# Two tokens per partition for q and k, another order of the loads, and more token halves in tile 1

## The chip, the cores and the metric

The kernel runs on one core of one Trainium2 chip. The metric is the device time of one execution in microseconds (us); before the change the median of five runs is 304.95 us (304.39 to 306.18). The engines are TensorE (PE, matrix multiplies), VectorE (DVE), ScalarE (ACT), GpSimd (POOL, which here issues the loads) and SyncE (SP, which issues the stores).

## The reference

What is computed is attention with a sliding window of 64 tokens, and then two layers with a SiLU between them on its result. There are 8 batches of 576 tokens (4608 in all), 8 heads of 64, d_model 512 and d_ff 2048. The inputs and the output are float32.

```python
rel = pos[:, None] - pos[None, :]
scores = np.where((rel >= 0) & (rel < 64), q @ k.T / sqrt(64), -1e9)
attn = softmax(scores) @ v                       # per batch and head
x = attn.transpose(0, 2, 1, 3).reshape(4608, 512)
h = x @ w_in
out = (h / (1 + exp(-h))) @ w_out
```

## The kernel before

Everything is one program whose order is made by a small planner in the kernel itself (the class `Plan`, lines 15 to 119). The functions `add_...` hand it operations with a class, an assumed duration for each engine that may run them, what they depend on, and, for work that writes PSUM, a pool of banks. `Plan.run` goes through an assumed time line: whenever an engine is free it takes, by rank, an operation whose dependencies have been seen. Then the operations are emitted in that order. The assumed durations are therefore costs in a plan; on the chip each engine runs its own list in order, and waits on semaphores where something is late. For a load that GpSimd issues, the plan adds to the transfer a time until it is seen: 1.2 us in the first 40 us of the plan, and 3.2 us after (line 102). No more than eight such loads are under way at once.

**Loads.** q, k, v, w_in and w_out are loaded by GpSimd's queue, which casts float32 to bfloat16 on the way; stores of the output go over SyncE. Batch 0's q and k come in large pieces and are turned by PE. For batches 1 to 7, `load_rows` (line 239) brings one head of q or k into 32 partitions of a `nat` tile: 18 tokens per partition, with partition p holding tokens p, 32 + p, 64 + p and so on. So the piece that lies together in DRAM is one token of one head, 64 elements. Four such loads fill one tile with four heads. `turn_blocks` (line 244) then has VectorE transpose it in blocks of 32 by 32 into `qt` or `kt`, in two instructions per tile: each takes half of the 18 token groups, and both halves of a head's 64 elements. A batch has four such tiles: q and k of heads 0 to 3 (group 0), q and k of heads 4 to 7 (group 1).

**Order of the loads.** After batch 0's inputs come the ten pieces of w_in. Then `SECOND_LOADS` (line 139) gives the order for batch 1, one letter at a time: `a` is q and then k of group 0 (eight loads), `b` those of group 1, `w` the next of the eight pieces of w_out (two d_ff blocks of 128 each), and `v` one of the four pieces of v. The pieces of w_out that are left follow. Later batches load `a`, `b` and then v. In this text w0 to w7 are the pieces of w_out and v0 to v3 those of batch 1's v.

**Attention.** A batch has three groups of 192 tokens. For each, PE makes the scores in four banks (48 small matmuls, line 333), ACT takes the exponent (line 339), VectorE applies the mask (line 342), and PE multiplies with v (48 small matmuls, line 351; called pv below). VectorE then takes a reciprocal (358), normalises (361) and transposes the result into `bridge` (365). The halves of v are first copied to a second place by VectorE (lines 299 and 301). PSUM has eight banks: `at` is banks 0 to 3, `mp` banks 4 to 7, and `pv` banks 4 and 5. In batch 1 pv takes its two banks from `at`, from batch 2 on from `pv` (line 508).

**The two layers.** Nine tiles of 512 tokens. In tile j, the first layer (line 371) makes 16 d_ff blocks, four matmuls of 512 tokens each, and ACT applies SiLU (line 377) from PSUM into a `g` tile. The second layer (line 380) has 64 matmuls: 16 d_ff blocks times four groups of 128 tokens. In tile 0 the d_ff blocks are the outer loop, so that w_out is used piece by piece, eight matmuls for each; all four `mp` banks are then held until the end. In tiles 0 and 1 the first `FIRST` = 6 d_ff blocks are made in two parts of the tokens, all first parts before all second parts, since the tokens of the second part come later out of attention: in tile 1 tokens 0 to 255 need the first group of batch 1, and tokens 256 to 511 all three. `add_tile` (line 530) writes this down in `work`.

PE's list in this part reads, in order: first layer of tile 0; second layer of tile 0, with the three score groups and the three pv of batch 1 in between; first layer of tile 1; then scores of batch 2 within the second layer of tile 1, and so on, tile by tile.

Of the kernel before, what the change touches and what calls it, by code (L numbers as in the profile page):

```python
# [14 lines left out]
class Plan:  # L15
# [31 lines left out]
    def run(self):  # L47
        head = {c: 0 for c in self.queues}
        engines = sorted({e for q in self.queues.values() for op in q for e in op["us"]})
        free = {e: 0.0 for e in engines}  # L50
        can = {e: [c for c, q in self.queues.items() if any(e in op["us"] for op in q)] for e in engines}
        table, left = "exp", self.count
        pipe, sent = {True: 1.8, False: 0.0}, []
        events, order = [0.0], []
        while left:
            if not events:
                raise RuntimeError([(c, head[c], q[head[c]]["n"]) for c, q in self.queues.items() if head[c] < len(q)])
            now = self.now = heapq.heappop(events)
            while events and events[0] == now:
                heapq.heappop(events)  # L60
            moved = True
            while moved:
                moved = False
                for e in engines:
                    if free[e] > now:
                        continue
                    best, kept = None, set()
                    heads = [(self.queues[c][head[c]], c) for c in can[e] if head[c] < len(self.queues[c])]
                    for op, c in sorted(heads, key=lambda x: x[0]["first"]):
                        if e == "POOL" and op["dma"] and len(sent) >= 8 and sent[-8] > now:  # L70
                            continue
                        if e not in op["us"] or not self.done(op["deps"]) or (op["gate"] and not op["gate"]()):
                            continue
                        if op["pool"]:
                            idle = [i for i in self.pools[op["pool"]] if i not in kept and self.done(self.banks[i])]
                            if len(idle) < len(op["untils"]):
                                if op["pool"] != "mp":
                                    kept.update(self.pools[op["pool"]])
                                continue
                            idle.sort(key=lambda i: (op["pool"] == "mp" and i in self.pools["pv"],  # L80
                                                     max([u["seen"] for u in self.banks[i]], default=0.0)))
                            op["bank"] = idle[:len(op["untils"])]
                            for i, until in zip(op["bank"], op["untils"]):
                                self.banks[i] = until
                        best = (op, c)
                        break
                    if best is None:
                        continue
                    op, c = best
                    head[c] += 1  # L90
                    us = op["us"][e]
                    if op["table"] and op["table"] != table:
                        table, us = op["table"], us + 1.28
                    end = free[e] = now + us
                    soft = e == "POOL"
                    if op["dma"] is None:
                        op["seen"] = end + op["lat"]
                    elif soft:

                        begin = max(pipe[True], end + 1.4)  # L100
                        pipe[True] = begin + op["dma"] * (1.5 if pipe[False] > begin else 1.0)
                        op["seen"] = pipe[True] + op["lat"] + (1.2 if now < 40 else 3.2)
                        sent.append(op["seen"])
                        heapq.heappush(events, op["seen"])
                    else:
                        begin = max(pipe[False], end + 1.0)
                        busy = pipe[True] > begin
                        pipe[False] = begin + op["dma"] * (1.6 if busy else 1.0)
                        if busy:
                            pipe[True] += 0.6 * op["dma"]  # L110
                        op["seen"] = pipe[False] + {"ld0": 1.2, "st": 1.2}.get(c, 3.0)
                    op["at"], op["cls"], op["by"] = now, c, e
                    order.append((op, e))
                    left -= c != "warm"
                    moved = True
                    heapq.heappush(events, end)
                    heapq.heappush(events, op["seen"])
        for op, e in order:
            op["fn"](e)
# [3 lines left out]
def kernel(ctx, tc, q, k, v, w_in, w_out, out):  # L123
    nc = tc.nc
    B, H, S, D = q.shape
# [1 line left out]
    assert (B, H, S, D) == (8, 8, 576, 64) and (d_model, d_ff) == (512, 2048)  # L127
    NP = H // 2
    NB = S // 64
    NR = S // 32  # L130
    NG = 3
    NDC = d_model // 128
    NFT = d_ff // 128
    TT = 512
# [1 line left out]
    TB = TT // 64  # L136
    NK = 2
    NN, NNB, NE, NOT, NGT = 8, 8, 12, 4, NFT + 3
    FIRST, SECOND_LOADS = 6, "awbwvwvvwv"
    FIRST_LOADS = [(x[0], int(x[1])) for x in "q0 k0 q1 k1 q2 q3 k2 k3 v0 v1 v2 v3".split()]  # L140
    NOX, NRC, NV = 6, 6, 3
    NIV = 2
    NM0, MARGIN = 9, 1.3
# [16 lines left out]
    nats = [keep.tile([128, 2 * S], BF16, name=f"nat{i}") for i in range(NN)]  # L160
# [15 lines left out]
    p = Plan(  # L176
        {"at": range(4), "pv": range(4, 6), "mp": range(4, 8), "all": range(8)},
        rank=dict(prime=-8, early=-10, one=-9, first=-9, dma=-1, ld0=-1, st=-2, silu=-3, out=-2, pv=0, s=1, moe=99, warm=200, turn=2,
                  norm=0, inverse=0, bridge=0, exp=1, mask=1, lift=2, block=2, shift=2, cast=4, late=5, clear=9),
        rank0=dict(turn=-6, cast=-6, lift=-5, shift=-4.5, exp=-4, mask=-4, inverse=-3.5, norm=-3, bridge=-3.2),  # L180
        ahead=dict(s=-5.5, exp=-4.6, pv=-5.5, inverse=-4.3, norm=-4.2, bridge=-4.25),
    )
# [55 lines left out]

    def load_rows(i, b, a, kk, h):
        nc.gpsimd.dma_start(  # L240
            out=nats[i][32 * h:32 * h + 32].rearrange("p (r d) -> p r d", r=NR),
            in_=(q, k)[kk][b, 4 * a + h].rearrange("(r p) d -> p r d", p=32))

    def turn_blocks(i, b, a, kk, part):

        n = NR // 2
        to = kt[b % NK][:, 64:] if kk else qt[b % NK]
        nc.vector.transpose(  # L248
            out=to[:, 2 * a * S:2 * a * S + 2 * S].rearrange("x (s r t) -> x s r t", s=2, r=NR)[:, :, n * part:n * part + n],
            in_=nats[i].rearrange("p (r s d) -> p s r d", r=NR, s=2)[:, :, n * part:n * part + n],  # L250
        )

    def load_v(e, b, part):
# [141 lines left out]
    kq_done, v_done, s_last, pv_last = {}, {}, {}, {}  # L395
    nat_free = {}
# [15 lines left out]
    n_nat = [0, 0]  # L412
# [31 lines left out]

    def add_batch_qk(b):
        busy = s_last.get(b - NK, []) + ([c_k[b % NK]] if b < NK else [])
        for what in SECOND_LOADS if b < NIV else "ab":
            if what == "w":
                add_w_out([len(wout)])
            elif what == "v":  # L450
                add_v_loads(b, [len(v_landed.get(b, []))], [c_vv[b]])
            else:
                add_four(b, "ab".index(what), busy)

    def add_four(b, a, busy):
        kq_done[(b, a)] = []
        for kk in range(2):
            i = n_nat[0] % NN
            n_nat[0] += 1
            ld = [p.add("dma", {"POOL": 0.72}, lambda _, i=i, kk=kk, h=h: load_rows(i, b, a, kk, h), nat_free.get(i, []),  # L460
                        dma=0.52, lat=MARGIN) for h in range(4)]
            nat_free[i] = [p.add("block", {"DVE": 0.75}, lambda _, i=i, kk=kk, part=part: turn_blocks(i, b, a, kk, part),
                                 ld + busy, b=b) for part in range(2)]
            kq_done[(b, a)] += nat_free[i]

    def add_v_loads(b, parts, busy):
        v_landed.setdefault(b, []).extend(
# [19 lines left out]
    def add_unit(b, g, which, n0):  # L487
        whole = b > 0
        first = "0" if b == 0 and g == 0 else ""
        na = len(which)  # L490
# [8 lines left out]
        for i in range(2 * na):  # L499
# [3 lines left out]
            if b:  # L503
# [1 line left out]
            ready.append(ex)  # L505
        g_mask.append(ready)
        pv = p.add("pv" + first, {"PE": 0.1 + 0.22 * na}, None, ready + [d for a in which for d in v_done[(b, a)]], lat=0.1,
                   pool="pv" if b > 1 else "at" if b else "all", b=b, nb=na)

        def run_values(_):  # L510
            for i, a in enumerate(which):
# [18 lines left out]
    def add_tile(j):  # L530
# [5 lines left out]
        if j == 0:  # L536
            work = [(ft, lo, hi) for lo, hi in ((0, 192), (192, TT)) for ft in range(FIRST)] + work[FIRST:]
        elif j == 1:
            work = [(ft, lo, hi) for lo, hi in ((0, 256), (256, TT)) for ft in range(FIRST)] + work[FIRST:]
        for i, (ft, lo, hi) in enumerate(work):  # L540
            have = [op for n in range((j * TT + hi + 191) // 192) for op in o_done[n]]
            g, si = gt[ft]
# [98 lines left out]
```

## Time and profile before

One execution was profiled. It took 304.39 us, the fastest of the five; its span, from the first instruction to the last, is 302.6 us. PE's granted clock is 1.00 in it throughout.

| What (profiled execution) | us |
|---|---|
| time of the execution | 304.39 |
| span | 302.6 |
| PE busy | 290.6 |
| DVE busy / ACT busy / POOL busy | 138.5 / 171.7 / 125.1 |
| second layer's matmuls (L380), 608 shown | 130.7 busy, 368 ns mean |
| first layer's matmuls (L371), 624 shown | 128.3 busy, 362 ns mean |
| SiLU (L377), 156 | 86.2 busy, 564 ns mean |
| q and k loads (L240), 112 issues, 72 KB each | 75.2 on POOL, 0.68 mean |
| v loads (L255), 32 issues, 144 KB each | 33.2 on POOL, 1.05 mean |
| transposes of q and k (L248), 56 | 39.6 on DVE, 0.75 mean |

How to read it: a matmul's duration runs from its start to its modelled end, while the next one starts before that; the second layer's follow each other at 0.2186 us (64 in 13.99 us). Sizes of loads are those of the bfloat16 that lands; twice as many bytes are read. Lines of a timeline give start, length, engine, line and operation, the tiles written and read, and how many instructions were merged; in brackets stands the idle time of the engine before them and what ended it. "DMA to landing" is counted from the start of the issuing instruction to the last of the transfer's completions.

### The profile page before, as it was taken

The numbers are of one execution on the slowest core, as the hardware profiler recorded it, in microseconds if no ns is written. First come the engines' busy times: TensorE is split into PE (matmuls) and PEld (weight loads), VectorE is DVE, ScalarE is ACT, GpSimd is POOL, SyncE is SP. The second block draws the span as 40 slices with busy tenths as digits, with TensorE's granted clock in tenths as the row PEclk, the third lists the DMA queues.
The fourth block names the chain that finished last, engine by engine and source line by source line (L and its number), as shares of the span: only waits on it lengthen the run. The fifth ranks groups of instructions, "written<-read, shape, count | busy, mean of one in ns | idle before, by whom it ended". The sixth has DMA issues, their size and how long they took to land.

```text
span 302.6 us, 8339 instructions
## 1 busy us (share of the span) xinstructions
PE 290.6 (96%) x3564; PEld 142.9 (47%) x3564; DVE 138.5 (46%) x330; ACT 171.7 (57%) x313; POOL 125.1 (41%) x177
## 2 busy tenths in 40 slices
PE   4999879999999999999999999999999999999996
PEld 2555334654544454445444454445444544444444
DVE  2592568843998198606960885066105520000000
ACT  4686462667357735774487538763767366226611
POOL 8966985989999979990320000000000000000000
PEclk9999999999999999999999999999999999999999
DMA  8999999999999999994490110001000110010012
GB/s 172 161 168 160 138 164 176 186 171 112 178 182 141 113 171 148 163 116 80 65 95 2 38 71 35 3 37 71 35 2 37 71 37 0 35 69 37 1 69 73
DMA packets 115238, 28.64 MB, mean 95 GB/s; under 512 B 104704, under 2 KB 110464, under 8 KB 115200
## 3 DMA queue, kind: packets, MB, share of 16 engines
q0 software_dynamic: 109440, 18.07, 79.5%
q1 hardware_dynamic: 5760, 10.03, 9.1%
q8 instruction: 28, 0.46, 0.6%
q14 instruction: 10, 0.08, 0.1%
HBM read 36.70 MB, written 9.44 MB: 152 GB/s over the span
## 4 chain that ended last, share of the span: by engine, by line
PE 83%; POOL 9%; DMA 6%; issue 1%; ACT 0%; POOLq 0%; ACTq 0%
PE mp L380 40%; PE mp L371 37%; DMA w_in_sb<-in_moe_w_in_dram 3%; PE at L333 3%; PE mp L351 3%; POOL vv L255 3%; DMA w_out_sb<-in_moe_w_out_dram 3%; POOL w_in_sb L261 2%; POOL nat L240 2%; POOL natb L230 1%; POOL w_out_sb L267 1%; PE at L351 0%; ACT g L377 0%; POOL ident L189 0%; ACT ot L386 0%
## 5 line engine op out<-in xcount | busy, mean ns | idle before, releaser
L380 PE MATMUL mp<-w_out_sb,g 128*128 128x512 bf16 (+2 forms) x608 | 130.7, 368 | 3.3 <-DMA w_out_sb<-in_moe_w_out_dram 3.3
L371 PE MATMUL mp<-bridge,w_in_sb 128*128 128x512 bf16 (+3 forms) x624 | 128.3, 362 | 1.4 <-DVE bridge L365 0.7
L377 ACT ACTIVATE g<-mp 128x512 bf16<-128x512 f32 (+3 forms) x156 | 86.2, 564 | 33.6 <-PE mp L371 32.5
L371 PEld LDWEIGHTS <-w_in_sb 128*128 128x128 bf16 x624 | 60.2, 97 | 67.9 <-issue 8.0
L380 PEld LDWEIGHTS <-g 128*128 128x128 bf16 x608 | 55.8, 98 | 63.1 <-issue 2.9
L386 ACT COPY ot<-mp 128x512 f32<-128x512 f32 (+2 forms) x36 | 20.1, 563 | 64.2 <-PE mp L380 51.0
L342 DVE TENSOR_TENSOR e<-e,mask 128x384 bf16<-128x384 bf16 x84 | 25.9, 349 | 61.5 <-ACT e L339 60.9
L339 ACT ACTIVATE e<-at 128x384 bf16<-128x384 f32 x90 | 37.2, 495 | 20.1 <-PE at L333 19.8
L240 POOL DMA_DIRECT2D nat<-in_k_dram x56 | 37.5, 678 | 10.8 <-DMA vv<-in_v_dram 3.1
L240 POOL DMA_DIRECT2D nat<-in_q_dram x56 | 37.7, 683 | 3.1 <-DMA w_in_sb<-in_moe_w_in_dram 2.1
L255 POOL DMA_DIRECT2D vv<-in_v_dram x32 | 33.2, 1050 | 12.6 <-PE mp L351 12.6
L365 DVE STREAM_TRANSPOSE bridge<-ox 128x384 bf16<-128x384 bf16 x48 | 24.7, 552 | 0.0
L248 DVE STREAM_TRANSPOSE qt<-nat 128x576 bf16<-128x576 bf16 x28 | 19.8, 747 | 7.8 <-DMA nat<-in_q_dram 7.8
L248 DVE STREAM_TRANSPOSE kt<-nat 128x576 bf16<-128x576 bf16 x28 | 19.8, 745 | 2.0 <-DMA nat<-in_k_dram 1.8
L361 DVE TENSOR_TENSOR ox<-mp,rc 128x384 bf16<-128x384 f32 x39 | 19.4, 537 | 0.1
L351 PEld LDWEIGHTS <-e 128*32 128x32 bf16 x1152 | 10.9, 95 | 9.7 <-issue 7.9
L358 DVE RECIPROCAL rc<-mp 128x6 f32<-128x6 f32 x39 | 7.3, 190 | 16.5 <-PE mp L351 15.9
L333 PEld LDWEIGHTS <-kt 32*128 32x128 bf16 x1008 | 9.3, 92 | 6.0 <-issue 5.4
L333 PE MATMUL at<-qt,kt 32*128 32x64 bf16 x1008 | 11.7, 190 | 0.0
L351 PE MATMUL mp<-vv,e 128*32 128x65 bf16 x936 | 11.1, 194 | 0.0
L339 ACT ACT_TABLE_LOAD x7 | 9.0, 1283 | 3.8 <-PE at L333 3.6
L301 DVE COPY vv<-vv 64x576 bf16<-64x576 bf16 (+1 forms) x14 | 8.3, 590 | 5.7 <-DMA vv<-in_v_dram 5.4
(50 smaller groups left out, 84.5 us busy)
## 6 DMA issues: line engine op xcount, KB each, us to landing
out_dram<-ot SPq DMA_DIRECT2D x35, 256.0 KB, 2.2
vv<-in_v_dram POOLq DMA_DIRECT2D x32, 144.0 KB, 5.1
nat<-in_q_dram POOLq DMA_DIRECT2D x56, 72.0 KB, 4.1
nat<-in_k_dram POOLq DMA_DIRECT2D x56, 72.0 KB, 3.6
w_out_sb<-in_moe_w_out_dram POOLq DMA_DIRECT2D x8, 256.0 KB, 7.1
w_in_sb<-in_moe_w_in_dram POOLq DMA_DIRECT2D x6, 256.0 KB, 8.2
w_in_sb<-in_moe_w_in_dram POOLq DMA_DIRECT2D x4, 128.0 KB, 4.7
natb<-in_q_dram POOLq DMA_DIRECT2D x3, 144.0 KB, 4.5
```

The costliest lines, as they stand in the source:

```text
L240: nc.gpsimd.dma_start(out=nats[i][32 * h:32 * h + 32].rearrange("p (r d) -> p r d", r=NR), in_=(q, k)[kk][b, 4 * a + h].rearrange("(r p) d ...
L248: nc.vector.transpose(out=to[:, 2 * a * S:2 * a * S + 2 * S].rearrange("x (s r t) -> x s r t", s=2, r=NR)[:, :, n * part:n * part + n], in ...
L255: queue[e].dma_start(out=vv[b % NV][:, 2 * g0 + 1:2 * g1 + 1:2, 0:D], in_=v[b].rearrange("h s d -> (h s) d").rearrange("(g p) d -> p g d", ...
L333: nc.tensor.matmul(at_six(op["bank"][h])[:, a, x], lhsT=kt[b % NK][r, at:at + 128], rhs=qt[b % NK][r, at:at + 64], start=(s == a == x == 0 ...
L339: nc.scalar.activation(out=es[n % NE], in_=at_six(bank), func=ACTF.Exp, scale=scale)
L342: nc.vector.tensor_mul(es[n % NE], es[n % NE], mask0 if g == 0 else mask)
L351: nc.tensor.matmul(at_pv(bank)[32 * h:32 * h + 32, x, t], lhsT=e_of(b, a, n, h)[:, x, 32 * t:32 * t + 32], rhs=vv[b % NV][:, (4 * a + h) * ...
L365: nc.vector.transpose(out=bridge[:, n0:n0 + 3, 2 * a:2 * a + 2].rearrange("x t s (u i) -> x t s u i", u=2), in_=oxs[n % NOX].rearrange("p ...
L371: nc.tensor.matmul(banks[bank["bank"][0]][:, lo:hi], lhsT=w_in_sb[:, c, ft * 128:(ft + 1) * 128], rhs=bridge[:, (j * TT + lo) // 64:(j * T ...
L377: nc.scalar.activation(out=gts[gt][:, lo:hi], in_=banks[bank["bank"][0]][:, lo:hi], func=ACTF.Silu)
L380: nc.tensor.matmul(banks[bank["bank"][0]][:, 0:hi - lo], lhsT=gts[gt][:, m * 128:(m + 1) * 128], rhs=w_out_sb[:, f, lo:hi], start=(f == 0) ...
L386: copies[e](out=ots[ot][:, lo:hi], in_=banks[bank["bank"][0]][:, 0:hi - lo])
```

## The change

Four things change.

1. `load_rows` and `turn_blocks`: a partition now gets two neighbouring tokens at a time (tokens 64 m + 2 p and 64 m + 2 p + 1 for m = 0 to 8), so 128 elements lie together in DRAM. The two transposes of a tile are now split by the half of a head's 64 elements; each still has 576 columns. A block's 32 transposed columns are written two elements apart, so that `qt` and `kt` hold the same values in the same places as before. The planner's costs of these operations are changed with them.
2. `SECOND_LOADS` names single tiles (0 and 1: q and k of group 0, 2 and 3: those of group 1). In batch 1 each is followed by a piece of w_out, and v follows later, in turn with w_out.
3. The planner takes a load that GpSimd issues to be seen 1.2 us after its transfer at any time.
4. In tile 1, 12 of the 16 d_ff blocks are made in token halves, in place of 6. And pv of batch 1's second and third group takes its banks from `pv`, as later batches do.

```diff
-                        op["seen"] = pipe[True] + op["lat"] + (1.2 if now < 40 else 3.2)
+                        op["seen"] = pipe[True] + op["lat"] + 1.2
...
-    FIRST, SECOND_LOADS = 6, "awbwvwvvwv"
+    FIRST, SPLIT, SECOND_LOADS = 6, 12, "0w1w2w3vwvwvwvww"
...
     def load_rows(i, b, a, kk, h):
         nc.gpsimd.dma_start(
-            out=nats[i][32 * h:32 * h + 32].rearrange("p (r d) -> p r d", r=NR),
-            in_=(q, k)[kk][b, 4 * a + h].rearrange("(r p) d -> p r d", p=32))
+            out=nats[i][32 * h:32 * h + 32].rearrange("p (m x) -> p m x", m=NB),
+            in_=(q, k)[kk][b, 4 * a + h].rearrange("(m p r) d -> p m (r d)", p=32, r=2))
 
     def turn_blocks(i, b, a, kk, part):
 
-        n = NR // 2
         to = kt[b % NK][:, 64:] if kk else qt[b % NK]
         nc.vector.transpose(
-            out=to[:, 2 * a * S:2 * a * S + 2 * S].rearrange("x (s r t) -> x s r t", s=2, r=NR)[:, :, n * part:n * part + n],
-            in_=nats[i].rearrange("p (r s d) -> p s r d", r=NR, s=2)[:, :, n * part:n * part + n],
+            out=to[:, (2 * a + part) * S:(2 * a + part + 1) * S].rearrange("x (m t r) -> x m r t", t=32, r=2),
+            in_=nats[i].rearrange("p (m r s d) -> p m r s d", m=NB, r=2, s=2)[:, :, :, part],
         )
...
-        for what in SECOND_LOADS if b < NIV else "ab":
+        for what in SECOND_LOADS if b < NIV else "0123":
...
-                add_four(b, "ab".index(what), busy)
+                add_four(b, *divmod(int(what), 2), busy)
...
+    def add_four(b, a, kk, busy):
+        i = n_nat[0] % NN
+        n_nat[0] += 1
+        ld = [p.add("dma", {"POOL": 0.6}, lambda _, h=h: load_rows(i, b, a, kk, h), nat_free.get(i, []),
+                    dma=0.42, lat=MARGIN) for h in range(4)]
+        nat_free[i] = [p.add("block", {"DVE": 0.79}, lambda _, part=part: turn_blocks(i, b, a, kk, part),
+                             ld + busy, b=b) for part in range(2)]
+        kq_done[(b, a)] = kq_done.get((b, a), []) + nat_free[i]
...
-                   pool="pv" if b > 1 else "at" if b else "all", b=b, nb=na)
+                   pool="pv" if b > 1 or (b, g) > (1, 0) else "at" if b else "all", b=b, nb=na)
...
-            work = [(ft, lo, hi) for lo, hi in ((0, 256), (256, TT)) for ft in range(FIRST)] + work[FIRST:]
+            work = [(ft, lo, hi) for lo, hi in ((0, 256), (256, TT)) for ft in range(SPLIT)] + work[SPLIT:]
```

The old `add_four` made q and k of a group in one call, with the costs 0.72 and 0.52 for a load and 0.75 for a transpose.

More of the change, by code (lines that the diff above doesn't have):

```diff
@@ L129 @@
     NB = S // 64
-    NR = S // 32
     NG = 3
@@ L452, in add_batch_qk @@
             else:
-                add_four(b, "ab".index(what), busy)
[L455 to L464, printed above, removed]
+                add_four(b, *divmod(int(what), 2), busy)
[7 more added lines that the diff above has]
+        kq_done[(b, a)] = kq_done.get((b, a), []) + nat_free[i]
     def add_v_loads(b, parts, busy):
```

## Prediction

> **What bounds the kernel now.** I read the page's busy times first, then TensorE's (PE's) instructions in order of time, then the chain of waits, GpSimd's issues, and last the rows of what is added.
>
> ```profile
> PE 290.6 (96%) x3564; PEld 142.9 (47%) x3564; DVE 138.5 (46%) x330; ACT 171.7 (57%) x313; POOL 125.1 (41%) x177
> DMA packets 115238, 28.64 MB, mean 95 GB/s; under 512 B 104704, under 2 KB 110464, under 8 KB 115200
> ```
>
> PE idles 12.0 of 302.6 us. The columns below are start, length, instructions; brackets hold the idle time before.
>
> ```profile
> 34.49 2.09 PE L380 MATMUL mp<-w_out_sb,g 128*128 128x512 bf16 x8
> 37.97 0.38 PE L380 MATMUL mp<-w_out_sb,g 128*128 128x512 bf16 x1 [1.40 <-DMA w_out_sb<-in_moe_w_out_dram]
> ...
> 41.05 1.89 PE L380 MATMUL mp<-w_out_sb,g 128*128 128x512 bf16 x8 [0.60 <-DMA w_out_sb<-in_moe_w_out_dram]
> ...
> 44.23 1.24 PE L380 MATMUL mp<-w_out_sb,g 128*128 128x512 bf16 x5 [0.81 <-DMA w_out_sb<-in_moe_w_out_dram]
> ...
> 47.18 0.59 PE L380 MATMUL mp<-w_out_sb,g 128*128 128x512 bf16 x2 [0.47 <-DMA w_out_sb<-in_moe_w_out_dram]
> ...
> 56.05 1.91 PE L371 MATMUL mp<-bridge,w_in_sb 128*128 128x256 bf16 x16
> 58.23 12.45 PE L371 MATMUL mp<-bridge,w_in_sb 128*128 128x256 bf16 x72 [0.28 <-ACT g L377]
> 70.62 0.55 PE L333 MATMUL at<-qt,kt 32*128 32x64 bf16 x48
> ```
>
> Tile 0's second layer eats w_out two d_ff blocks (eight matmuls) at a time, and waits four times for a piece: 3.28 us. From 58.2 on PE has no gap until 279. So only what ends tile 1's first layer (70.6) earlier or later moves the end. The chain of waits names the wait that decides:
>
> ```profile
> 39.45 7.69 DMA w_out_sb<-in_moe_w_out_dram
> 47.13 0.04 issue
> 47.18 0.59 PE mp L380 x2
> ```
>
> That is the fifth piece (w4). And GpSimd's timeline says that the transfers, not their issue, are short there: each issue waits for an older landing.
>
> ```profile
> 44.48 0.66 POOL L240 DMA_DIRECT2D nat<-in_q_dram x1 [0.57 <-DMA w_out_sb<-in_moe_w_out_dram]
> ...
> 47.42 0.66 POOL L240 DMA_DIRECT2D nat<-in_k_dram x1 [1.23 <-DMA w_out_sb<-in_moe_w_out_dram]
> ```
>
> Landings (issue plus time to landing of each DMA in the trace): the last w_in piece 26.35; w0 to w7 at 31.83, 37.93, 41.01, 44.19, 47.13, 48.61, 49.50, 51.01; batch 1's v at 39.17, 42.02, 42.95, 45.16. Differences of neighbours are prices of a transfer in the full queue: q/k 0.47 (eight in 3.68, eight in 3.86 us), v 1.04, w_out 1.62 in the mean: 1.82 for the five behind smaller transfers, 1.29 for the three behind another w_out. Test: 26.35 + 16 x 0.47 + 4 x 1.04 + 8 x 1.62 = 51.0, and w7 landed at 51.01.
>
> **The change, part by part.**
>
> *Two tokens per partition.* A q/k load has 288 packets of 512 bytes read in place of 576 of 256. Per engine the old 36 packets take 0.47 us, 13.1 ns each; the first loads (L230) have 8 packets of 2304 bytes per engine and land 0.70 apart, 88 ns each. The line through both gives 22.4 ns for 512 bytes, times 18: 0.40 us. Bounds: 0.36 (bytes at L230's rate, half of 0.70) and 0.47 (nothing gained). I take 0.40, as both rows bracket the new packet. The Trainium skill (DMA: Bandwidth & Descriptors, Specifications) speaks against this: under 512 bytes a packet doesn't reach line rate, as the engine reads, modifies and writes. The written side, in bf16, grows only from 128 to 256 bytes, so by that rule the new packets stay on the slow side, as the 104704 short ones of the page are; the sum by it would have 0.47, 1.1 us later.
> Issuing: between L230's 0.53 us (128 packets) and 0.65 now; free, since GpSimd idles for landings in this stretch, and where it doesn't (52 to 62) no one waits for it.
>
> *Transposes (L248).* Same 576 columns, but written 4 bytes apart. No row has such a write; L365 reads 4 bytes apart: 384 columns in 0.552 us against L248's 576 in 0.747, so 1.02 ns for each further column and no sign of a price for the step. Bounds: 0 and, at twice that per column, 0.6 us more each. I take 0. Loads of batch 1 arrive a pair of transposes per 3.3 us (four q/k and a w_out), so 1.5 us of transposing is covered.
>
> *Order of the loads.* After w_in come q, w0, k, w1, q, w2, k, w3 (v0 before it) and so on, w6 right after v3, w7. No load is dropped; w1 to w4 are moved past q/k of their own batch and v past w_out. w6 lands at 26.35 + 16 x 0.40 + 4 x 1.04 + 7 w. For w: 1.62 the mean, 1.82 if small neighbours are its cause, since all seven now follow small ones. Part of that 0.2 is small packets' tails, counted already; I take 1.72, so 12.04 and w6 at 48.95 (1.62: 48.25; 1.82: 49.65). Scores of batch 1 move behind 24 of tile 0's matmuls (9 now); their k lands about 37 against 35.69, needed at 40. v3, at 47.2 against 45.16, needs 0.7 us of copies (L301, L299), just ahead of the first pv at 49.2.
>
> *PE after w6.* PE has only 48 matmuls and three scores to do before it: 34.5 + 48 x 0.2186 + 1.45 = 46.4, so w6 decides (w7, 1.3 to 1.7 later, finds the eight matmuls of w6, 1.75 us, and a pv before it). Behind it are 16 matmuls (3.50) and one pv (0.49); in the old run 32 matmuls and three pv (8.47 by such prices) took 8.84, so 0.12 per pv for switching. Tile 0 ends at 48.95 + 0.05 + 3.50 + 0.49 + 0.12 = 53.1, not 56.02.
>
> *Tile 1 and pv's banks.* Tile 1's first layer took 56.05 to 70.69, 14.64. Added: two pv of batch 1 with their switching, 1.22; 48 more half matmuls. 32 halves and 40 whole ones took 12.45: 12.45 - 40 x 0.2186 = 3.71, 0.116 per half, 0.0066 above half a whole one: 0.32. And a wait: pv of batch 1's second and third group now use banks 4 and 5 of the four that the first layer uses, until they are normalised. Silu starts late (a table load stands before it):
>
> ```profile
> 56.50 1.28 ACT L377 ACT_TABLE_LOAD   x1
> 57.80 4.51 ACT L377 ACTIVATE g<-mp 128x256 bf16<-128x256 f32 x12
> ```
>
> Two banks hold 0.93 us of halves, four 1.9; the difference, 0.9, is unfilled but for one pv (0.61): 0.3; then each pair of halves takes 0.46 + 0.38 and two hops against 0.93, about 0.1 more, twice or so. Together 0.5. Bounds: 0 (DVE frees the banks early) and 1.5 (0.28 idle now, five times).
> Twelve more silu pieces keep ACT under PE: 24 x 0.38 + 4 x 0.6 = 11.5 us in some 15.
>
> *The planner's 1.2 us after 40 us.* It only changes the order; DVE gets seven of batch 3's transposes ahead of batch 2's first normalisations. Those loads landed by 73.96, DVE needs them at 74.4, and they come about 3 us earlier (w7 1, 24 loads 0.07 each): free. If they don't, PE stands at the pv at 76.
>
> *Sum.* Tile 1's first layer ends at 53.1 + 0.03 + 14.64 + 1.22 + 0.32 + 0.50 = 69.8, against 70.69: -0.9 us. The rest of PE's work is the same. The profiled execution took 304.39 us (302.6 span, 1.8 around it), so 303.5 there; it was the fastest of five, 0.56 under the median of 304.95. Predicted median: 304.05 us.
>
> **Rivals.** *The gain is eaten in tile 1, or the rows are only as fast as before: no change.* With 0.47 the sum is +0.2; with a bank wait of 1.5 it is +0.1. For it: ACT ends PE's waits at 20 and 58 already. Against: banks 4 and 5 are freed in 2.1 us of DVE work per pv. About 305.1.
> *All transfers get cheaper, w_out too:* if tails of small packets made w_out 1.82, fewer of them give 1.62 and 0.38: 16 x 0.02 + 7 x 0.10 = 1.0 earlier, 303.05. For it: w_in's 512 KB reads landed 1.3 apart. Against: 1.97 behind v, which stays.
> *Alternating costs (slower).* Every w_out behind small packets takes the mean of its four dearest rows, 1.96 (1.80, 2.24, 1.84, 1.97), as engines that still hold small packets hold back a landing; with q/k at 0.43 that is -0.9 + 7 x 0.24 + 16 x 0.03 = +1.3, so 306.2 at the wait for w6. It passes +0.9 from w = 1.91. Against: the whole queue fits 1.62.
> *Transposes at twice the time per column:* batch 3's seven cost DVE 4.2 us before 76; idle DVE time (10.2 of 22 us from 52 to 74) takes part; some 2 us on PE, 306.1.
>
> **How the numbers follow.** 0.3% (0.9 us) is about what a measurement of this kernel can tell from no change, and the forecast stands on that bound: 0.40, half of it faster, half within. Cheaper transfers: 0.22, so faster 0.42. Gain eaten: 0.15, so no change 0.35. Alternating 0.12 and transposes 0.11: slower 0.23. Low end: w 1.62, q/k 0.36 and no bank wait, -0.9 - 0.7 - 0.64 - 0.5 = -2.7, and 302.4 leaves out little of it. High end: 306.2 by alternating, 306.3 with some of the transposes. The likeliest case alone: 303.2 to 304.9.
>
> **What would show it.** Right: q/k landings 0.40 apart, w6 near 49, PE's last wait for w_out at w6, tile 1's first layer ending near 69.8, L248 at 0.74 us, no gap on PE later. Wrong: a wait of PE for DVE between 70 and 80, w_out pieces 1.9 apart, or q/k at 0.47.

## The result, and the profile after

The changed kernel takes 303.16 us in the median (30 runs, 301.32 to 304.46) against 304.41 (56 runs) for the kernel before. The ratio is 0.9952, 95% interval 0.9939 to 0.9965, or 1.5 us less (0.0048 x 304.41; interval 1.1 to 1.9); the two medians stand 1.25 us apart. The prediction had 0.9 us less, and its range held the time. Of the 0.89 us between its 304.05 and the 303.16, 0.54 are the starting point: its 304.95 was a median of five runs. The executions that were profiled took 304.39 us (before, at its median) and 301.73 us (after, 1.4 below its own), so the difference of the two traces, 2.6 us, is larger than that of the medians.

The page after, busy times, packets, and the row of a transpose:

```profile
PE 290.0 (97%) x3588; PEld 145.0 (48%) x3588; DVE 137.2 (46%) x330; ACT 173.0 (58%) x319; POOL 118.0 (39%) x177
DMA packets 82982, 28.64 MB, mean 95 GB/s; under 512 B 72448, under 2 KB 78208, under 8 KB 82944
...
L246 DVE STREAM_TRANSPOSE qt<-nat 128x576 bf16<-128x576 bf16 x28 | 20.7, 787 | 6.0 <-DMA nat<-in_q_dram 6.0
```

PE is busy as long as before to 0.6 us; 32,256 packets are gone, half of the 64,512 that q and k had. The same stretch of TensorE's (PE's) timeline as before the change, with the idle time before an instruction in brackets (in this kernel L380, L371, L333 and L351 are L378, L369, L331 and L349):

```profile
34.13 5.54 PE L378 MATMUL mp<-w_out_sb,g 128*128 128x512 bf16 x24
39.60 0.55 PE L331 MATMUL at<-qt,kt 32*128 32x64 bf16 x48
40.08 1.90 PE L378 MATMUL mp<-w_out_sb,g 128*128 128x512 bf16 x8
42.48 0.59 PE L378 MATMUL mp<-w_out_sb,g 128*128 128x512 bf16 x2 [0.50 <-DMA w_out_sb<-in_moe_w_out_dram]
...
51.53 0.60 PE L369 MATMUL mp<-bridge,w_in_sb 128*128 128x256 bf16 x4
...
53.72 1.56 PE L369 MATMUL mp<-bridge,w_in_sb 128*128 128x256 bf16 x11 [0.56 <-ACT g L375]
55.20 0.56 PE L349 MATMUL mp<-vv,e 128*32 128x65 bf16 x48
55.70 12.33 PE L369 MATMUL mp<-bridge,w_in_sb 128*128 128x256 bf16 x93
67.96 0.55 PE L331 MATMUL at<-qt,kt 32*128 32x64 bf16 x48
```

Four waits for w_out (3.28 us) have become one of 0.50. Tile 0's second layer and what stands in it last 17.41 us (34.13 to 51.53) in place of 21.56; tile 1's first layer 16.42 (to the scores at 67.96) in place of 14.57, since two pv (0.49 each) have moved into it, 24 matmuls have become 48 halves, and it waits longer for ACT. Together 2.30 us are gone. From those scores to PE's end it is 229.1 us in both. The other 0.36 was there at the start of tile 0's second layer already (34.13 against 34.49). The chain of waits, as before the change, names the fifth piece of w_out, w4:

```profile
36.08 6.36 DMA w_out_sb<-in_moe_w_out_dram
42.44 0.04 issue
42.48 0.59 PE mp L378 x2
```

It lands at 42.44, not 47.13. Ahead of it the chain goes back through GpSimd's issues, as it did before the change, where it reads:

```profile
26.63 0.66 POOL nat L240
27.30 0.73 POOL w_out_sb L267
28.02 5.28 POOL nat L240 x8
33.31 0.71 POOL w_out_sb L267
...
38.55 0.90 POOL vv L255
```

GpSimd issued there from 26.63 to 43.91 without a pause, a q/k load every 0.65 us, and the issue of w4 came at 39.45. In the changed kernel it comes at 36.08. Of the 4.7 us by which w4 lands earlier, 1.0 is an earlier start of this run of issues in the trace (25.63, as the last piece of w_in landed 1.0 sooner), 2.4 is what no longer stands ahead of w4 in GpSimd's list or is issued faster, and 1.3 is a shorter time from issue to landing (6.36 for 7.69).

### The profile page after: what moved, and what is told of

It reads as the page before. It is cut to its first block, busy times and chain, and to the rows that moved or that the text cites. A ratio compares the mean times of both kernels' runs of the same rounds, so it can differ in the third digit from the quotient of the medians.

```text
span 300.0 us, 8386 instructions
## 1 busy us (share of the span) xinstructions
PE 290.0 (97%) x3588; PEld 145.0 (48%) x3588; DVE 137.2 (46%) x330; ACT 173.0 (58%) x319; POOL 118.0 (39%) x177
## 4 chain that ended last, share of the span: by engine, by line
PE 83%; POOL 8%; DMA 5%; issue 1%; DVE 1%; ACT 1%; POOLq 0%; ACTq 0%; DVEq 0%
PE mp L378 40%; PE mp L369 37%; PE at L331 3%; PE mp L349 3%; DMA w_in_sb<-in_moe_w_in_dram 3%; POOL w_in_sb L259 2%; DMA w_out_sb<-in_moe_w_out_dram 2%; POOL nat L239 2%; POOL vv L253 2%; POOL natb L229 1%; POOL w_out_sb L265 1%; ACT g L375 0%; DVE ot L384 0%; PE at L349 0%; DVE qt L246 0%
## 5 line engine op out<-in xcount | busy, mean ns | idle before, releaser
L369 PE MATMUL mp<-bridge,w_in_sb 128*128 128x512 bf16 (+3 forms) x648 | 129.0, 355 | 1.7 <-DVE bridge L363 0.7
L378 PE MATMUL mp<-w_out_sb,g 128*128 128x512 bf16 (+2 forms) x608 | 130.1, 368 | 0.5 <-DMA w_out_sb<-in_moe_w_out_dram 0.5
L375 ACT ACTIVATE g<-mp 128x512 bf16<-128x512 f32 (+3 forms) x162 | 87.6, 550 | 34.1 <-PE mp L369 32.3
L369 PEld LDWEIGHTS <-w_in_sb 128*128 128x128 bf16 x648 | 62.4, 97 | 66.1 <-issue 8.2
L378 PEld LDWEIGHTS <-g 128*128 128x128 bf16 x608 | 56.0, 98 | 62.0 <-issue 1.1
L239 POOL DMA_DIRECT2D nat<-in_k_dram x56 | 34.2, 617 | 12.8 <-DMA vv<-in_v_dram 7.1
L253 POOL DMA_DIRECT2D vv<-in_v_dram x32 | 31.9, 1005 | 13.6 <-PE mp L349 12.8
L239 POOL DMA_DIRECT2D nat<-in_q_dram x56 | 34.7, 632 | 3.2 <-DMA w_in_sb<-in_moe_w_in_dram 1.5
L246 DVE STREAM_TRANSPOSE qt<-nat 128x576 bf16<-128x576 bf16 x28 | 20.7, 787 | 6.0 <-DMA nat<-in_q_dram 6.0
L246 DVE STREAM_TRANSPOSE kt<-nat 128x576 bf16<-128x576 bf16 x28 | 20.6, 783 | 5.2 <-DMA nat<-in_k_dram 5.2
L359 DVE TENSOR_TENSOR ox<-mp,rc 128x384 bf16<-128x384 f32 x43 | 21.4, 537 | 0.1
L349 PEld LDWEIGHTS <-e 128*32 128x32 bf16 x1152 | 10.9, 95 | 9.4 <-issue 7.9
L299 DVE COPY vv<-vv 64x576 bf16<-64x576 bf16 (+1 forms) x14 | 7.5, 536 | 13.6 <-DMA vv<-in_v_dram 8.4
L349 PE MATMUL mp<-vv,e 128*32 128x65 bf16 x1032 | 12.4, 194 | 0.0
L331 PE MATMUL at<-qt,kt 32*128 32x64 bf16 x1008 | 11.7, 190 | 0.0
L331 PEld LDWEIGHTS <-kt 32*128 32x128 bf16 x1008 | 9.4, 92 | 4.5 <-issue 3.4
```

The lines of the kernel that those rows point to most:

```text
L239: nc.gpsimd.dma_start(out=nats[i][32 * h:32 * h + 32].rearrange("p (m x) -> p m x", m=NB), in_=(q, k)[kk][b, 4 * a + h].rearrange("(m p r) ...
L246: nc.vector.transpose(out=to[:, (2 * a + part) * S:(2 * a + part + 1) * S].rearrange("x (m t r) -> x m r t", t=32, r=2), in_=nats[i].rearr ...
L253: queue[e].dma_start(out=vv[b % NV][:, 2 * g0 + 1:2 * g1 + 1:2, 0:D], in_=v[b].rearrange("h s d -> (h s) d").rearrange("(g p) d -> p g d", ...
L331: nc.tensor.matmul(at_six(op["bank"][h])[:, a, x], lhsT=kt[b % NK][r, at:at + 128], rhs=qt[b % NK][r, at:at + 64], start=(s == a == x == 0 ...
L349: nc.tensor.matmul(at_pv(bank)[32 * h:32 * h + 32, x, t], lhsT=e_of(b, a, n, h)[:, x, 32 * t:32 * t + 32], rhs=vv[b % NV][:, (4 * a + h) * ...
L359: nc.vector.tensor_mul(oxs[n % NOX], at_pv(bank)[:, :, :, 0:D], rcs[n % NRC].unsqueeze(3).to_broadcast([128, 3, 2, D]))
```

## The experiments

Three explanations were set against each other. A: the order of the loads makes the gain, by landing w_out's first pieces earlier, with the longer run of token halves as a cover for the later pv; the rows only make each q/k load a little shorter. B: fewer packets make it. C: token halves and banks in tile 1 make it. The next table is worked out from each kernel's trace: from the first matmul of tile 0's second layer to the first of tile 1's first layer (I), from there to batch 2's first scores (II), from there to PE's end (III), and PE's waits in I and II.

| Kernel | ratio to before, 95% | I | II | III | w_out waits | other waits of PE in I and II |
|---|---|---|---|---|---|---|
| before | 1 | 21.56 | 14.57 | 229.10 | 3.28 | ACT 0.28 |
| rows_alone | 0.9988 (0.9962 to 1.0014) | 19.54 | 14.57 | 229.51 | 1.53 | ACT 0.28 |
| order_alone | 1.0004 (0.9978 to 1.0031) | 19.64 | 16.83 | 229.26 | 1.23 | bridge 1.27, kt 0.31, ACT 0.28 |
| tile1_alone | 1.0011 (0.9988 to 1.0033) | 19.55 | 16.23 | 229.52 | 2.12 | ACT 0.56 |
| all_but_rows | 0.9970 (0.9948 to 0.9992) | 19.72 | 16.42 | 228.94 | 0.90 | kt 1.30, ACT 0.56 |
| all_but_order | 1.0041 (1.0017 to 1.0065) | 19.11 | 16.42 | 230.28 | 2.16 | ACT 0.56 |
| all_but_tile1 | 0.9980 (0.9962 to 0.9998) | 18.57 | 16.41 | 229.54 | 1.10 | bridge 0.65, ACT 0.48 |
| all_but_seen | 0.9942 (0.9921 to 0.9963) | 18.48 | 16.42 | 229.04 | 1.55 | ACT 0.56 |
| changed | 0.9952 (0.9939 to 0.9965) | 17.41 | 16.42 | 229.11 | 0.50 | ACT 0.56 |
| pv_in_at | 0.9922 (0.9900 to 0.9945) | 18.01 | 15.47 | 229.03 | 0.17 | bridge 0.65, ACT 0.20 |

One trace is one execution: the start of I lies between 33.4 and 35.5 us in these ten although the work up to it is the same. What ends a wait for a load doesn't depend on that start, so I gets shorter when PE comes late; the ratios, not these lengths, decide.

One number doesn't depend on PE: how long after the last piece of w_in a piece of w_out landed. For w4 that is 20.16 to 20.78 us in the four kernels with the old order, and 17.05 to 17.38 in the six with the new one. With the old order it is 20.78 and 20.16 with one-token rows, 20.60 and 20.54 with two; with the new order 17.37 and 17.38 with one, 17.05 to 17.38 with two. So the order lands w4 some 3.3 us earlier, and for the rows no gain shows there.

**rows_alone.** The new `load_rows` and `turn_blocks`, and their costs in the planner; all else as before.

```diff
-            in_=(q, k)[kk][b, 4 * a + h].rearrange("(r p) d -> p r d", p=32))
+            in_=(q, k)[kk][b, 4 * a + h].rearrange("(m p r) d -> p m (r d)", p=32, r=2))
```

> The kernel before with two-token rows alone (and their costs in the planner); old order of the loads, 6 d_ff blocks in halves, pv of batch 1 in at. Theory A (the order of the loads, with the longer run of token halves as its cover, makes the gain; rows only give 0.05 us per q/k load while TensorE waits for w_out): q/k land 0.42 apart, TensorE still waits some 3 us for w_out over four waits, the fifth piece lands 16 x 0.05 = 0.8 us earlier: -0.8 us, ratio 0.997. Theory B (fewer packets make the gain): the whole -1.4 us, ratio 0.995. Theory C (token halves and banks in tile 1 make it): 0.

Measured: 0.9988, and the interval has 1 in it. B isn't what happened. A's size is right within the interval; the waits for w_out fell more than it said (1.53 us, two waits), for PE began I a microsecond later here, and the last piece of w_in landed 0.86 us sooner.

**order_alone.** The order of batch 1's loads alone.

```diff
-    FIRST, SECOND_LOADS = 6, "awbwvwvvwv"
+    FIRST, SECOND_LOADS = 6, "0w1w2w3vwvwvwvww"
```

> The kernel before with the new order of batch 1's loads alone; one-token rows, 6 d_ff blocks in halves, pv of batch 1 in at. Theory A: waits for w_out shrink from 3.3 to about 1.5 us, but the third pv now stands later, so that after 12 halves (2 x 6 blocks) TensorE waits about 1 to 1.7 us for VectorE's last bridge: in all -0.8 to +0.3 us. If alternating made w_out pieces dear, they land 1.9 apart and the time is over +0.9. Theory B: 0 or slower. Theory C: 0.

Measured: 1.0004. Two lines of PE's waits (who waited for whom, us in total, times, longest) show where the gain goes:

```profile
PE mp L371 <- DVE bridge L365: 1.3, 1, 1.3
PE mp L380 <- DMA w_out_sb<-in_moe_w_out_dram: 1.2, 1, 1.2
```

The waits for w_out are 2.0 us shorter, but after the first halves of six d_ff blocks (24 matmuls) PE needs the tokens of batch 1's third group, and stands 1.27 us for its bridge, which comes after a pv that now stands in tile 1. The wait has moved. w_out pieces landed 1.35 us after their forerunners in the mean; that alternating makes them dear (1.9) is refuted.

**tile1_alone.** Token halves and banks alone.

```diff
-    FIRST, SECOND_LOADS = 6, "awbwvwvvwv"
+    FIRST, SPLIT, SECOND_LOADS = 6, 12, "awbwvwvvwv"
...
-                   pool="pv" if b > 1 else "at" if b else "all", b=b, nb=na)
+                   pool="pv" if b > 1 or (b, g) > (1, 0) else "at" if b else "all", b=b, nb=na)
...
-            work = [(ft, lo, hi) for lo, hi in ((0, 256), (256, TT)) for ft in range(FIRST)] + work[FIRST:]
+            work = [(ft, lo, hi) for lo, hi in ((0, 256), (256, TT)) for ft in range(SPLIT)] + work[SPLIT:]
```

> The kernel before with 12 d_ff blocks in halves and pv of batch 1's later groups in pv banks; old loads. Theory A: w_out waits stay at 3 us; 48 more half matmuls cost 0.3 and a wait for ACT 0.5, and one pv moves into tile 1: 0 to +0.6 us. Theory C: -1.4 us, ratio 0.995.

Measured: 1.0011, no gain that can be told. C falls as the sole cause. The loads are those of the kernel before, and yet the waits for w_out are 2.12 us in this trace, not 3.28: the last piece of w_in landed 0.72 us earlier. So much can one trace differ from another.

**all_but_rows.** The changed kernel with one-token rows: the first diff turned round.

> The changed kernel with one-token rows. Theory A: waits for w_out grow from 0.5 to about 1.5 us, q/k land 0.47 apart: 0.3 to 0.8 us of the gain is lost, so -0.6 to -1.1 against before, ratio 0.996 to 0.998. Theory B: no gain is left, 1.000. Theory C: all of it is left, 0.995.

Measured: 0.9970. Order and tile 1 together (with the planner's 1.2 us, of which all_but_seen shows no effect) give about 0.9 us where neither gives any that can be told alone; the intervals overlap a little, and it is the wait for a bridge, 1.27 us in order_alone and gone here, that makes the difference plain. That rows add to it isn't shown by the ratios (0.9970 and 0.9952, with overlapping intervals). PE waits less for w_out here (0.90) than for k's transposes (1.30), as scores of batch 1 stand behind k. But of the 2.36 us by which k landed later than in the changed kernel, 1.52 are a later last piece of w_in in this trace; order_alone, with the same one-token rows, waited 0.31.

**all_but_order.** The changed kernel with the old order, `"awbwvwvvwv"` and q and k of a group in one call.

> The changed kernel with the old order of batch 1's loads (q and k of group 0, w_out, q and k of group 1, and so on). Theory A: TensorE waits again some 2.5 to 3 us for w_out, in four waits; rows give -0.8 and the halves and bank waits +0.3 to +0.8: -0.5 to 0 us against before, ratio 0.998 to 1.000. Theories B and C: the gain stays, 0.995.

Measured: 1.0041, slower than before. Waits for w_out are back (2.16 us in three). But III is 1.2 us longer too, and that was in no expectation. VectorE's timeline in tile 2, and below it PE's:

```profile
108.53 1.12 DVE L340 TENSOR_TENSOR e<-e,mask 128x384 bf16<-128x384 bf16 x4
112.90 0.75 DVE L299 COPY vv<-vv 64x2304 bf16<-64x2304 bf16 x1 [3.26 <-DMA nat<-in_k_dram]
113.69 0.27 DVE L356 RECIPROCAL rc<-mp 128x6 f32<-128x6 f32 x2
...
115.81 1.12 DVE L340 TENSOR_TENSOR e<-e,mask 128x384 bf16<-128x384 bf16 x4
```

```profile
116.18 1.35 PE L349 MATMUL mp<-vv,e 128*32 128x65 bf16 x48 [0.26 <-DVE e L340]
```

A copy of v stands at the head of VectorE's list, 3.26 us idle, since v's last piece lands at 112.78 (the view's inference says k; no k lands then); behind it wait a normalisation and the masks, and PE's pv starts late and then runs with small gaps, 1.35 us in place of 0.56. In this list the planner put the copy ahead of the masks. That the shorter time until a load is seen did that is likely: before, rows_alone and tile1_alone have this order with the old time, and their III is 229.10 to 229.52. But no run differs from this one in that alone.

**all_but_tile1.** The changed kernel with 6 blocks in halves and pv of batch 1 in `at`: the tile 1 diff turned round.

> The changed kernel with 6 d_ff blocks of tile 1 in halves and pv of batch 1 in at. Theory A: few waits for w_out (0.5 us), but TensorE waits 0.6 to 1.5 us for the third group's bridge before the second token parts: -0.3 to -0.9 us against before. Theory C: no gain is left, 1.000. Theory B: 0.995.

Measured: 0.9980, 0.6 us less than before, in the middle of A's range, with 0.65 us of waiting for a bridge and 1.10 for w_out, where A had 0.5. The interval (0.9962 to 0.9998) leaves out both C's 1.000 and B's 0.995.

**all_but_seen.** The changed kernel with the old time until a load is seen.

```diff
-                        op["seen"] = pipe[True] + op["lat"] + 1.2
+                        op["seen"] = pipe[True] + op["lat"] + (1.2 if now < 40 else 3.2)
```

> The changed kernel with the planner's old time until a load is seen (3.2 us after the first 40). Only the order in which some transposes and masks stand on VectorE differs, and those loads land early: all theories say no difference from the changed kernel, 0.995. If the later part had been bound by VectorE, 0.99 or 1.00.

Measured: 0.9942, as the changed kernel; III is 229.04. In the changed kernel this part does nothing to the time that can be told.

**pv_in_at.** The changed kernel with all pv of batch 1 in `at`; 12 blocks stay in halves.

```diff
-                   pool="pv" if b > 1 or (b, g) > (1, 0) else "at" if b else "all", b=b, nb=na)
+                   pool="pv" if b > 1 else "at" if b else "all", b=b, nb=na)
```

> The changed kernel with pv of all of batch 1 in banks of at (so that the first layer of tile 1 has all four of its banks); 12 blocks in halves stay. The prediction's bank wait says: the wait for ACT at the start of tile 1 (0.56 us in the changed kernel) stays if the late table load alone makes it, and goes if two banks are too few; 0 to -0.5 us against the changed kernel, ratio 0.9935 to 0.995. If pv in at is held back by batch 2's scores, slower.

Measured: 0.9922, 2.4 us less than before (0.0078 x 304.6), a little less than the changed kernel; the intervals just overlap, so this isn't settled. PE's timeline at the start of tile 1:

```profile
52.90 0.38 PE L369 MATMUL mp<-bridge,w_in_sb 128*128 128x256 bf16 x2
53.92 1.36 PE L369 MATMUL mp<-bridge,w_in_sb 128*128 128x256 bf16 x11 [0.65 <-DVE bridge L363]
55.21 0.56 PE L349 MATMUL at<-vv,e 128*32 128x65 bf16 x48
55.70 12.73 PE L369 MATMUL mp<-bridge,w_in_sb 128*128 128x256 bf16 x99
```

The wait for ACT is gone from here, and one for a bridge stands in its place, 0.65 for 0.56. One pv has moved back from II to I. But the first layer itself runs faster: without its pv it takes 14.98 us in place of 15.44. The 11 matmuls behind the wait take 1.29 us here (53.92 to 55.21) and 1.48 in the changed kernel (53.72 to 55.20), and there a further stop of 0.26 us follows behind the pv, which the changed kernel's chain of waits puts to ACT:

```profile
55.76 0.23 PE mp L369
...
56.07 0.39 ACT g L375
...
56.51 11.52 PE mp L369 x88
```

The lengths come back: II is 16.42 in changed, all_but_rows, all_but_order and all_but_seen, and 15.47 in pv_in_at and in three_tokens_pv_in_at below. So pv in banks 4 and 5 costs tile 1 some 0.46 us, and this part of the change is a loss there. I and II together, 33.48 against 33.83, say less, since PE came to I 0.76 us later here.

**six_tokens and eighteen_tokens.** The changed kernel with 6 or 18 tokens per partition together, to part the price of a packet from that of a byte, and to see the price of the step in the transposes' writing.

```diff
-            in_=(q, k)[kk][b, 4 * a + h].rearrange("(m p r) d -> p m (r d)", p=32, r=2))
+            in_=(q, k)[kk][b, 4 * a + h].rearrange("(m p r) d -> p m (r d)", p=32, r=6))
...
-            out=to[:, (2 * a + part) * S:(2 * a + part + 1) * S].rearrange("x (m t r) -> x m r t", t=32, r=2),
+            out=to[:, (2 * a + part) * S:(2 * a + part + 1) * S].rearrange("x (m t r) -> x m r t", t=32, r=6),
```

The other two lines follow with `m=3`; with eighteen tokens it is `r=18` and `m=1`.

> The changed kernel with six neighbouring tokens per partition (96 packets of 1536 bytes read and 768 written per q/k load); transposes write 12 bytes apart. By the prediction's line (3.7 ns and 0.0366 ns a byte, per packet and engine) a load takes 6 x 59.9 = 0.36 us against 0.42 measured with two tokens: w_out lands 0.06 us per earlier q/k load sooner, 0.5 to 1 us in all, but only one wait of 0.5 us for w_out is left in the changed kernel: 0 to -0.5 us against it, ratio 0.9935 to 0.995. The Trainium skill's 512-byte rule (DMA: Bandwidth & Descriptors, Specifications) would have a larger step here than from one token to two, since only now both sides are over 512 bytes: well under 0.36. For the transposes the trace has 0.747 us with 2 bytes apart and 0.785 with 4: if that is a price per byte of step, 0.94 now; if a fixed one, 0.785.

> The changed kernel with all 18 tokens of a partition together (32 packets of 4608 bytes read per q/k load); transposes write 36 bytes apart. Line: 2 x 172 ns = 0.34 us per load, hardly less than with six tokens, since bytes set it. Transposes: at a price per byte of step 1.4 us, at a fixed one 0.785. With 1.4 VectorE has 34 us more work and the time is over +1 us against before; with 0.785 it is as with six tokens.

Measured: 1.0535 (1.0499 to 1.0570) and 1.1428 (1.1397 to 1.1460). The rows of the transposes, first six tokens, then eighteen:

```profile
L246 DVE STREAM_TRANSPOSE kt<-nat 128x576 bf16<-128x576 bf16 x28 | 57.7, 2191 | 0.0
L246 DVE STREAM_TRANSPOSE qt<-nat 128x576 bf16<-128x576 bf16 x28 | 57.1, 2173 | 5.8 <-DMA nat<-in_q_dram 5.7
```

```profile
L246 DVE STREAM_TRANSPOSE kt<-nat 128x576 bf16<-128x576 bf16 x28 | 73.7, 2798 | 0.0
L246 DVE STREAM_TRANSPOSE qt<-nat 128x576 bf16<-128x576 bf16 x28 | 72.8, 2768 | 4.8 <-DMA nat<-in_q_dram 4.8
```

2.18 us and 2.78 us for what takes 0.785 with two tokens. Neither price that was expected is right: not fixed, and much steeper than the 0.02 us per byte from one token to two. The transposes read the same way in all of these; what differs is the step of their write. VectorE holds PE up: PE waits 7.0 us for k and 4.7 for masks with six tokens, 13.9 and 17.5 with eighteen. Not all of the loss is waiting: the granted clock was 0.973 and 0.955 in these traces, and PE was busy 299.7 and 302.8 us, not 290.0. The loads, which were to be measured, differ little (below).

**six_tokens_pv_in_at.** Six tokens on pv_in_at, sent together with the two before it.

> The kernel with pv of all of batch 1 in at (0.9922) with six tokens per partition. If loads still end waits of TensorE there (0.17 us), and VectorE isn't slower, 0 to -0.3 us against it: 0.991 to 0.9925. If transposes at a wider step cost VectorE more than 0.15 us each, later pv wait for it, and the ratio is above 0.995.

Measured: 1.0589 (1.0562 to 1.0616), transposes of 2.19 us: the same waits again.

**three_tokens_pv_in_at.** Three tokens (`r=3` in both places) on pv_in_at.

> The kernel with pv of all of batch 1 in at (0.9922) with three neighbouring tokens per partition (192 packets of 768 bytes per q/k load); transposes write 6 bytes apart. Measured so far per transpose: 0.747 us at 2 bytes, 0.785 at 4, 2.18 at 12, 2.78 at 36. The Trainium skill (SBUF - State Buffer, Door 1) says that two or more accesses to the same 16-byte line go at full rate: 6 bytes gives 2.7 a line, so about 0.8 us, and a time as with two tokens, 0.990 to 0.9945. If the price rises evenly from 4 to 12 bytes it is 1.13 us, which VectorE's idle time covers but for the scores of batch 1: 0.993 to 0.998. If any step that isn't a power of two costs what 12 bytes do, 2.2 us and over 1.04. Loads: 0.36 to 0.42 us.

Measured: 0.9928 (0.9901 to 0.9955), as with two tokens, and

```profile
L246 DVE STREAM_TRANSPOSE qt<-nat 128x576 bf16<-128x576 bf16 x28 | 29.7, 1122 | 6.0 <-DMA nat<-in_q_dram 6.0
L246 DVE STREAM_TRANSPOSE kt<-nat 128x576 bf16<-128x576 bf16 x28 | 29.5, 1116 | 2.2 <-DMA nat<-in_k_dram 2.2
```

1.12 us: the price rises evenly from 4 to 12 bytes, as the second guess had it. VectorE's idle time covers 56 x 0.33 = 19 us of it.

## Why the prediction was right, step by step

- *What bounds it, and where the time would come from.* Right: waits for w_out fell from 3.28 to 0.50 us, tile 1's first layer ended earlier, and the rest is 229.1 us of PE in both. Over the traces the waits were 1.53 to 3.28 us with the old order and 0.17 to 1.55 with the new one, so the two traces show the fall at its largest. The runs add what the sum hid: order and tile 1 give nothing that can be told apart (1.0004, 1.0011) and 0.9970 together, because order alone turns the wait for w_out into one for the bridge.
- *A q/k load, 0.40.* 0.415 in the mean of 16 (0.47 before). Right in size; over the other traces the means are 0.42 to 0.53 with two tokens and 0.48 to 0.58 with one, the medians over all traces 0.42 to 0.45 and 0.48 to 0.55. The sum made 16 x 0.07 = 1.1 us of it at w6. Counted from the last piece of w_in, w6 landed at 22.27 and 22.79 us with the new order and one token, and at 21.72 to 22.24 with two, some 0.6 earlier; at w4 no gain shows.
- *Issuing, free.* A wrong reading. The lines that it rests on, where each issue waits for an older landing, begin at 44.48; from 26.63 to 43.91, where half of batch 1's q and k, its v and all of w_out are sent, GpSimd never paused. From 27.99 to 32.60 each q/k load landed sooner after its issue than the one before it, 4.34 falling to 3.09 us: issues 0.65 apart were slower than transfers 0.47 apart. From w1's issue on the time to landing grows (4.68 to 9.40), and there transfers are short. Two-token rows shorten the issue too, to 0.59. No run parts that from the shorter transfer, so which of them would be the gain of the rows stays open.
- *w_out pieces, 1.72 each.* The term that was mis-sized. The first seven took 1.54 in the mean, seven times 0.18 less: w6 was worked out at 48.95 and landed at 47.06, 1.89 earlier: 7 x 0.18 = 1.26 of it from this, 1.01 from the last w_in piece, which landed at 25.34 and not at 26.35, and 0.4 the other way from q/k and v. In all six kernels with the new order the first seven took 1.25 to 1.63. So the 0.1 that was added to 1.62 was wrong in its direction: w_out that alternates with small packets isn't dearer. That its landing takes in what they leave, as the prediction says, was argued and not measured.
- *The deciding landing, w6.* Wrong in place: PE's last wait was for w4. With pieces that early, PE had enough to do. Tile 0 ended at 51.5, not at 53.1. In all_but_rows, where all landed later, PE's last wait was for w6 (49.65).
- *Tile 1's first layer.* Worked out as 14.64 + 1.22 + 0.32 + 0.50 = 16.68, measured 16.42, and ACT's wait 0.56. Right in size. That the banks make the wait of 0.56 was argued, and pv_in_at, where as long a wait for a bridge stands at that spot, doesn't show it; but there the layer is 0.46 us shorter without its pv, against the 0.50 of the sum.
- *Transposes, nothing.* 0.038 us more each (0.747 to 0.785), 2 us in all on VectorE and nothing on PE. The bound of 0.6 was the right thing to keep: against one token's 0.747, three tokens add 0.37 and six 1.4.
- *The planner's 1.2 us, free.* Free in the changed kernel (all_but_seen). The queue it named, VectorE's, did make PE wait in all_but_order, there behind a copy of v.
- *Rivals.* Cheaper transfers has the better price, w_out 1.62 where 1.54 came. Its 303.05 us is close to the 303.16 by luck: it is 1.9 us under a start of 304.95 that came out as 304.41. As a gain it had 1.9 and the likeliest case 0.9, and 1.5 by the ratio, 1.25 by the medians, lies between them. Alternating is refuted by the prices, transposes at twice the time by 0.785.

## What to carry to other kernels

When several loads share one queue, ask for each consumer which landing it waits for next, and move that load forward; then ask at once which consumer of the load that moved back is next, since here the order alone gained nothing that could be told, as PE then stood for the tokens of tile 1. Look also at which is slower in each stretch, the engine that issues the loads or the transfers. Longer runs in DRAM are bought with a step in some later write: measure that price at each length before taking the next, as it may be nothing at two tokens and the whole kernel at six. And judge a change of half a per cent by many runs: single traces differed by two microseconds at a point up to which PE's work is the same.

## What the runs showed of the hardware

- **A transpose's write step on VectorE.** 128x576 in bfloat16, written 2, 4, 6, 12 and 36 bytes apart: 0.747, 0.785, 1.12, 2.18 and 2.78 us. From 4 to 12 bytes that is 0.17 us a byte. The Trainium skill (SBUF - State Buffer, in the section on Door 1) says that accesses are at full rate while two or more fall into the same 16-byte line, and gives 8 bfloat16 as the step that is free. At 4 bytes the trace agrees to 0.04 us; at 6 bytes, 2.7 accesses a line, it doesn't (1.12 us), and 12 bytes cost 2.9 times the contiguous write. The measurement decides here.
- **Small packets.** Batch 1's 16 q/k loads, the same bytes each, landed apart by 0.48 to 0.55 us with 256 bytes read per packet (medians of four traces), 0.42 to 0.45 with 512 (six), 0.39 with 768 (one), 0.36 and 0.39 with 1536 (two) and 0.35 with 4608 (one). The means are 0.47 to 0.58, 0.415 to 0.53, 0.385, 0.41 and 0.435, and 0.356, as single landings of 0.9 to 1.8 us weigh on them. The prediction's line gave 0.47, 0.40, 0.38, 0.36 and 0.34. The Trainium skill (DMA: Bandwidth & Descriptors, Specifications) says that a transfer needs at least 512 bytes for line rate. Taken of the written side, that would put a step between 768 and 1536 bytes read, and taken of the read side one at 512; neither place shows a step larger than the line's.
- **GpSimd's issues.** A q/k load was issued 0.65 us after the one before it with 576 packets, 0.59 to 0.60 with 288, 0.56 with 192 and with 96, and 0.51 with 32 (medians of the time from one start to the next).
- **Something that stays open.** The last w_in piece, whose load was not changed, landed at 25.63 to 26.86 us in four traces with one-token rows and at 25.25 to 25.57 in six with two tokens, as if the small packets queued behind it held it back; with three and eighteen tokens it was 25.49 and 25.31, but with six 26.06 and 26.23. No run separated this.
